# An expert's first layer begun with 128 rows, behind filler products, in an mLSTM and hash-routed mixture kernel

## Chip, cores and metric

The kernel runs on one core of a Trainium2 chip. The time is that of the whole program on the device, in microseconds: 430.01 us before the change, the median of three runs (429.15 to 430.22).

## What is computed

Two blocks follow each other. The first is an mLSTM cell over 4 batches, 8 heads and 768 time steps, with head dimension 40. Its output becomes a matrix x of 3072 rows (tokens) and 320 columns. The second sends each row to one of 8 experts by a hash of its token id; an expert is two matrix products with a relu between.

```python
def _moe_ref(x, token_ids, w1, w2):
    expert_idx = token_ids * np.int64(2654435761) % np.int64(E)
    for e in range(E):
        mask = expert_idx == e
        xe = x[mask]
        h = np.maximum(xe @ w1[e], 0.0)   # 320 -> 1024
        out[mask] = h @ w2[e]             # 1024 -> 320
```

All values are float32.

## The kernel before

**Attention.** The 3072 rows are worked in 24 blocks of 128 time steps (NT = 24, `s` in the loop), chunk by chunk with a carried state. TensorE (PE) makes the scores (L351), the part from the state (L402) and the part from the block (L409), and the transposes back (L424, tile xo). `finish(s)` normalises a block: VectorE (DVE) makes a denominator (L430, L433), multiplies by the output gate (L436, the last reader of xo in PSUM), takes a reciprocal (L439), and GpSimd (POOL) multiplies (L440). Then the sync queue stores 128 rows of x to DRAM (L441). Routing tables, which say what token lies in what slot of what expert, are made beside it.

**Experts.** Each of 8 experts takes 416 slots (CAP): three tiles of 128 rows and 32 of a remainder tile, `xr`, which four experts share. `fetch(e)` gathers rows of x from DRAM with an indirect DMA issued by POOL (L790), one for each tile, 3 for an expert and a fourth for xr at experts 0 and 4. As the rows were written by attention, the first gather waits for the last store. `turns(e)` is a list of four pieces: three that transpose a tile (`turn`, L806 on: two transposes L810, a small VectorE copy of the last 64 columns, L811, a third transpose L812, and a copy from PSUM to xT by VectorE, L816, or ScalarE, L814), and `remainder`, which at expert 0 transposes xr into `remT` (copied by ScalarE) and then copies 32 of its columns into xT on POOL (L896).

`layer1` goes over the 1024 hidden columns in four pairs of 128 (`fp`). Each has four whole matmuls (L834; 128 rows of w1, two for each half of the pair) and two halves (L827; the last 64 rows of w1, packed so that two run side by side in the array's row halves), into two PSUM tiles `mh`, of which there are four. VectorE evicts one with a relu (L841), ScalarE the other (L843). An fp32 matmul appears as two passes in the trace, so the eight passes of a pair's whole matmuls are one group. `layer2` multiplies h with w2 (L863, tile zp), and each 128 rows are copied by ScalarE (L796) and scattered by POOL (L797). Between the pairs of `layer1` and the tiles of `layer2` the function `between` is called: it puts the turns of the next expert into PE's order, and the issue of expert 2's weights (`third`, on ScalarE's queue).

The order of the work is written out by hand: each engine runs its instructions in the order in which the program names them, and semaphore waits are derived from the tiles. For expert 0 all four turns stand ahead of `layer1`. The PSUM pools of attention and of the experts use the same banks, so the first tiles of the second wait for readers of the first.

Of the kernel before, what the change touches and what calls it, by code (L numbers as in the profile page):

```python
# [8 lines left out]
F32 = mybir.dt.float32  # L9
# [4 lines left out]
AF = mybir.ActivationFunctionType  # L14
ALU = mybir.AluOpType
PSUM = bass.MemoryType.PSUM

P = 128
# [4 lines left out]
def kernel(  # L23
# [24 lines left out]
    nc = tc.nc  # L48
    B, H, S, D = q.shape
# [4 lines left out]
    E, _, F = moe_w1.shape  # L54
    FB = F // P
    NT = N // P
    PR = H // 2
# [9 lines left out]
    RM = 32  # L67
    EG = P // RM
    NM = NJ * P
    CAP = NM + RM  # L70
# [11 lines left out]
    ident = consts.tile([P, P], F32, name="ident")  # L82
# [20 lines left out]
    W = {}  # L103
# [13 lines left out]
    with tc.tile_pool(name="gates", bufs=1) as gp, \  # L117
# [308 lines left out]
        def finish(s):  # L426
            d = st.pop(s)
            hs = d["xo"].rearrange("p f i (x d) -> p f (i x) d", d=DP)
            den = wk.tile([P, 2, PR, 1], F32, name="den")
            nc.vector.tensor_scalar(  # L430
                den[:], hs[:, :, :, D:D1], scalar1=-1.0, scalar2=1.0, op0=ALU.mult, op1=ALU.max,
            )
            nc.vector.tensor_tensor(den[:], den[:], hs[:, :, :, D:D1], op=ALU.max)  # L433
            x = wk.tile([P, H, D], F32, name="x")
            xv = x.rearrange("p (j f) d -> p f j d", f=2)
            nc.vector.tensor_tensor(  # L436
                xv, hs[:, :, :, :D], og[s].rearrange("p (j f) d -> p f j d", f=2), op=ALU.mult,
            )
            nc.vector.reciprocal(den[:], den[:])  # L439
            nc.gpsimd.tensor_tensor(xv, xv, den[:].to_broadcast([P, 2, PR, D]), op=ALU.mult)  # L440
            return lambda: nc.sync.dma_start(x_d[s * P : (s + 1) * P, :], x.rearrange("p h d -> p (h d)"))  # L441


# [168 lines left out]
        one = gp.tile([P, 2, 1], F32, name="one")  # L612
# [174 lines left out]
    mps = ctx.enter_context(tc.tile_pool(name="mps", bufs=2, space=PSUM))  # L787

    def gather(xg, idx):
        nc.gpsimd.indirect_dma_start(  # L790
            out=xg, out_offset=None, in_=x_d[:, :], in_offset=bass.IndirectOffsetOnAxis(ap=idx, axis=0),
        )
# [13 lines left out]
    def turn(xg, dst, on_act):  # L806

        tp = mps.tile([P, DB, P], F32, name="tp")
        for db in range(2):
            nc.tensor.transpose(tp[:, db, :], xg[:, db * P : (db + 1) * P], ident[:])  # L810
        nc.vector.tensor_copy(xg[:, Dm:], xg[:, 2 * P : Dm])  # L811
        nc.tensor.transpose(tp[:, 2, :], xg[:, 2 * P :], ident[:])  # L812
        if on_act:
            nc.scalar.copy(dst, tp[:])  # L814
        else:
            nc.vector.tensor_copy(dst, tp[:])  # L816

    def layer1(w, xT, h, cols, between=lambda fp: None):

        w1t, w1c, _ = w  # L820
        for fp in range(FB // 2):
            hp = [mps.tile([P, CAP], F32, name="mh", bufs=4) for _ in range(2)]

            def halves(first):
                for i in range(2):
                    r = slice(i * P // 2, (i + 1) * P // 2)
                    nc.tensor.matmul(  # L827
                        hp[i][:, :cols], lhsT=w1c[r, fp, :], rhs=xT[r, 2, :cols], start=first, stop=not first,
                    )

            def whole(i, first):
                fb = 2 * fp + i
                for db in range(2):
                    nc.tensor.matmul(  # L834
                        hp[i][:, :cols], lhsT=w1t[:, db, fb * P : (fb + 1) * P], rhs=xT[:, db, :cols],
                        start=(first and db == 0), stop=(not first and db == 1),
                    )

            def out(i):
                if i == 0:  # L840
                    nc.vector.tensor_relu(h[:, 2 * fp, :cols], hp[i][:, :cols])  # L841
                else:
                    nc.scalar.activation(h[:, 2 * fp + 1, :cols], hp[i][:, :cols], AF.Relu)  # L843

            if fp % 2 == 0:
                for i in range(2):
                    whole(i, True)
                between(fp)
                halves(False)
                for i in range(2):  # L850
                    out(i)
            else:
                halves(True)
                for i in range(2):
                    whole(i, False)
                    out(i)
                between(fp)
# [12 lines left out]
    def cols_of(t, c0):  # L870
        return lambda j: t[:, c0 + j : c0 + j + 1]

    with tc.manual_schedule():
        xgs, xTs, remT, hrem = {}, {}, {}, {}

        def fetch(e):
            if e % EG == 0:
                xgs[-1 - e // EG] = xp.tile([P, DB * P], F32, name="xr")
            xgs[e] = xp.tile([P, NJ, DB * P], F32, name="xg", bufs=3)
            for j in range(NJ):  # L880
                gather(xgs[e][:, j, :Dm], cols_of(g_idx, e * NJ)(j))
            if e % EG == 0:
                gather(xgs[-1 - e // EG][:, :Dm], cols_of(g_idx, NR + e // EG)(0))

        def turns(e):
            xT = xTs[e] = xp.tile([P, DB, CAP], F32, name="xT")

            def tile_of(j):
                turn(xgs[e][:, j, :], xT[:, :, j * P : (j + 1) * P], j % 2 == 1)

            def remainder():
                i = e % EG
                if i == 0:
                    remT[e // EG] = xp.tile([P, DB, P], F32, name="remT")
                    turn(xgs[-1 - e // EG], remT[e // EG][:], True)
                nc.gpsimd.tensor_copy(xT[:, :, NM:], remT[e // EG][:, :, i * RM : (i + 1) * RM])  # L896

            return [lambda j=j: tile_of(j) for j in range(NJ)] + [remainder]

        def rest(g):  # L900
            zp = mps.tile([P, Dm], F32, name="zp")
            for fb in range(FB):
                for i in range(EG):
                    nc.tensor.matmul(
                        zp[i * RM : (i + 1) * RM, :], lhsT=hrem[g][:, i, fb, :], rhs=W[g * EG + i][2][:, fb, :],
                        start=(fb == 0), stop=(fb == FB - 1),
                    )
            scatter(zp, cols_of(s_idx, NR + g)(0), True)

        fetch(0)  # L910
        fetch(1)

        third = weight_slices(2)
        for piece in turns(0):
            piece()
        for e in range(E):
            g, i = e // EG, e % EG
            if e + 2 < E:
                fetch(e + 2)
            h = xp.tile([P, FB, CAP], F32, name="h")  # L920
            if i == 0:
                hrem[g] = xp.tile([P, EG, FB, RM], F32, name="hrem")
            ahead = turns(e + 1) if e + 1 < E else []

            def one(_):
                if ahead:
                    ahead.pop(0)()
                for _ in range(3):
                    if third:
                        third.pop(0)(nc.scalar)  # L930

            def after(j):
                one(j)
                if j == 0 and i == EG - 1:
                    rest(g)

            layer1(W[e], xTs[e], h, CAP, one)
            nc.gpsimd.tensor_copy(hrem[g][:, i], h[:, :, NM:])  # L938
            layer2(W[e], h, NJ, cols_of(s_idx, e * NJ), True, after)
            if e + 3 < E:  # L940
                load_weights(e + 3)

    nx = nc.values_load(xe[0:1, NX : NX + 1], min_val=0, max_val=NX)
    with tc.If(nx > 0):
        with tc.For_i(0, nx, 1) as k:
            ex = nc.sync.value_load(xe[0:1, bass.ds(k, 1)], min_val=0, max_val=E - 1)
            gs = xp.tile([P, 2], I32, name="gs")
            nc.vector.tensor_copy(gs[:, 0:1], g_idx[:, bass.ds(k + (NC - NX), 1)])
            nc.vector.tensor_copy(gs[:, 1:2], s_idx[:, bass.ds(k + (NC - NX), 1)])
            w, slices = weights(  # L950
                moe_w1[bass.ds(ex, 1)].rearrange("e d f -> (e d) f"),
                moe_w2[bass.ds(ex, 1)].rearrange("e f d -> (e f) d"), wpools[0], w2pools[0],
            )
            for piece in slices:
                piece()
            xr = xp.tile([P, DB * P], F32, name="xr")
            xT = xp.tile([P, DB, CAP], F32, name="xT")
            h = xp.tile([P, FB, CAP], F32, name="h")
            gather(xr[:, :Dm], gs[:, 0:1])
            turn(xr, xT[:, :, :P], False)  # L960
            layer1(w, xT, h, P)
            layer2(w, h, 1, lambda j: gs[:, 1:2], False)


# [28 lines left out]
```

## Time and profile before

The profiled execution has a span of 427.9 us. Busy times:

| engine | busy us | share |
|---|---|---|
| PE (matmul) | 386.1 | 90% |
| PEld (weight load, beside PE) | 258.5 | 60% |
| DVE | 136.1 | 32% |
| ACT (ScalarE) | 134.6 | 31% |
| POOL | 118.7 | 28% |

The page cuts the span into 40 slices and gives each engine's busy share in tenths, and the clock that PE was granted (9 is full). The chain that ended last is followed back from the last instruction, through what released each. Groups have a line, an engine, an output and its inputs, and the mean duration of one; a duration of a matmul includes its way through the array, so that successive ones overlap and their distance, not their duration, is their cost. "issue" is time in which an engine waited for nothing that the profile shows.

Expert 0's layer 1 stands between 173 and 198 us of the span. Of the costliest groups, the whole matmuls of `layer1` (L834) take 98.9 us in 256 passes, those of `layer2` (L863) 105.2 us in 384, the halves (L827) 26.7 us in 128.

### The profile page before, as it was taken

How to read it: one execution, taken by the hardware profiler on the slowest of the kernel's cores; microseconds unless marked ns; L12 is line 12 of the kernel's file. 1: busy time of each engine (PE TensorE's matmuls, PEld its weight loads, DVE VectorE, ACT ScalarE, POOL GpSimd, SP SyncE). 2: the span in 40 equal slices, each digit the busy share in tenths (PEclk: the TensorE clock that was granted, in tenths of full speed). 3: DMA queues.
4: the chain of work that ended last, by engine and by line, in shares of the span. 5: the costliest groups of instructions: out<-in, count | busy, mean ns of one | idle time of the engine just before them, and what ended most of it. 6: DMA issues, size and time to landing. Idle time of an engine off the chain costs nothing.

```text
span 427.9 us, 7402 instructions
## 1 busy us (share of the span) xinstructions
PE 386.1 (90%) x2862; PEld 258.5 (60%) x2862; DVE 136.1 (32%) x371; ACT 134.6 (31%) x238; POOL 118.7 (28%) x204
## 2 busy tenths in 40 slices
PE   2369999999999992599999999999999999999992
PEld 2257867877887871356656557556556566575551
DVE  7464748766675761211020120110110210201100
ACT  5158776686495471011010110110111111111010
POOL 6363323313323422710321501302302312021021
PEclk9868999999999998589999999999999999999997
DMA  8929998899676720527616318235216201000000
GB/s 168 213 61 172 206 218 180 190 205 214 149 161 129 161 90 33 163 96 239 193 46 212 120 29 271 62 98 170 75 64 214 61 8 38 0 15 31 1 17 30
DMA packets 111784, 51.37 MB, mean 120 GB/s; under 512 B 86624, under 2 KB 105892, under 8 KB 111748
## 3 DMA queue, kind: packets, MB, share of 16 engines
q1 hardware_dynamic: 105898, 39.31, 38.2%
q0 software_dynamic: 2496, 8.20, 6.0%
q10 hardware_dynamic: 3354, 3.37, 2.4%
q8 instruction: 23, 0.38, 0.4%
q14 instruction: 13, 0.11, 0.1%
HBM read 42.00 MB, written 8.63 MB: 118 GB/s over the span
## 4 chain that ended last, share of the span: by engine, by line
PE 78%; issue 5%; ACT 5%; DMA 4%; POOL 2%; DVE 1%; SPq 1%; ACTq 0%; POOLq 0%; DVEq 0%
PE mh L834 22%; PE zp L863 21%; PE mh L827 6%; PE sp L351 6%; PE ht L409 6%; PE ht L402 3%; PE ab L311 2%; PE tr L275 2%; PE xo L424 2%; PE ht L382 2%; PE tk L588 1%; PE tp L810 1%; ACT qT L289 1%; PE xb L323 1%; PE tr L288 1%
## 5 line engine op out<-in xcount | busy, mean ns | idle before, releaser
L863 PE MATMUL zp<-w2t,h 128*128 128x320 f32 x384 | 105.2, 433 | 0.0
L834 PE MATMUL mh<-xT,w1t 128*128 128x416 f32 x256 | 98.9, 531 | 0.9 <-POOL xT L896 0.9
L863 PEld LDWEIGHTS zp<-w2t,h 128*128 128x128 f32 x384 | 72.7, 190 | 32.1 <-issue 3.3
L834 PEld LDWEIGHTS mh<-xT,w1t 128*128 128x128 f32 x256 | 47.8, 194 | 44.0 <-issue 41.6
L816 DVE COPY xT<-tp 128x384 f32<-128x384 f32 x16 | 8.9, 558 | 142.3 <-PE tp L812 124.7
L797 POOL DMA_INDIRECT out_dram<-zo,s_idx x26 | 25.6, 986 | 92.5 <-ACT zo L796 92.5
L843 ACT ACTIVATE h<-mh 128x416 f32<-128x416 f32 x32 | 16.6, 517 | 110.1 <-PE mh L827 60.3
L796 ACT COPY zo<-zp 128x320 f32<-128x320 f32 x26 | 11.1, 426 | 101.1 <-PE zp L863 92.9
L841 DVE TENSOR_SCALAR h<-mh 128x416 f32<-128x416 f32 x32 | 18.9, 592 | 53.4 <-PE mh L834 26.9
L359 DVE TENSOR_TENSOR w<-sp,w 128x512 f32<-128x512 f32 x48 | 30.9, 686 | 13.8 <-PE sp L351 10.3
L440 POOL TENSOR_TENSOR x<-x,den 128x320 f32<-128x320 f32 x24 | 17.4, 724 | 64.0 <-DVE den L439 34.1
L351 PE MATMUL sp<-qT,kT 64*128 64x128 f32 x384 | 29.7, 297 | 4.1 <-ACT qT L289 4.1
L351 PEld LDWEIGHTS sp<-qT,kT 64*128 64x128 f32 x384 | 24.9, 199 | 10.8 <-ACT qT L289 6.0
L315 ACT ACTIVATE w<-ab 128x512 f32<-128x512 f32 x48 | 26.6, 611 | 5.0 <-PE ab L311 4.9
L409 PE MATMUL ht<-w,v 128*64 128x128 f32 x384 | 27.1, 285 | 0.0
L827 PE MATMUL mh<-xT,w1c 64*128 64x416 f32 x128 | 26.7, 535 | 0.0
L938 POOL COPY hrem<-h 128x256 f32<-128x256 f32 x8 | 3.2, 400 | 84.1 <-ACT h L843 84.1
L790 POOL DMA_INDIRECT xg<-x_rows,g_idx x24 | 23.4, 976 | 9.7 <-issue 9.7
L417 ACT COPY hT<-ht 128x512 f32<-128x512 f32 x24 | 14.1, 587 | 31.2 <-PE ht L409 31.2
L409 PEld LDWEIGHTS ht<-w,v 128*64 128x64 f32 x384 | 21.2, 140 | 4.0 <-issue 3.1
L289 ACT COPY qT<-tr 128x512 f32<-128x512 f32 x24 | 22.9, 975 | 0.6 <-PE tr L288 0.3
L275 PE MATMUL tr<-ident,k 128*128 128x128 f32 x96 | 17.2, 307 | 4.3 <-DMA k<-in_k_dram 4.3
(177 smaller groups left out, 407.0 us busy)
## 6 DMA issues: line engine op xcount, KB each, us to landing
w2t<-in_moe_w_dram SPq DMA_DIRECT2D x28, 320.0 KB
w1t<-in_moe_w_dram SPq DMA_DIRECT2D x28, 256.0 KB
k<-in_k_dram SPq DMA_DIRECT2D x24, 160.0 KB
v<-in_v_dram SPq DMA_DIRECT2D x24, 160.0 KB
og<-in_o_gate_dram SPq DMA_DIRECT2D x24, 160.0 KB
x_rows<-x SPq DMA_DIRECT2D x24, 160.0 KB
ql<-in_q_dram SPq DMA_DIRECT2D x6, 480.0 KB
w1c<-in_moe_w_dram SPq DMA_DIRECT2D x14, 128.0 KB
```

What stands on the lines that cost most here:

```text
L275: nc.tensor.transpose(tp[:, j, :], d["k"][:, 2 * j : 2 * j + 2, :].rearrange("p h d -> p (h d)"), ident[:])
L289: nc.scalar.copy(qb[b]["T"][:, :, cols], tp[:])
L315: nc.scalar.activation(w[:, hf], ab[:], AF.Exp)
L351: nc.tensor.matmul(sp[hf][:, j, :], lhsT=d["kT"][r, j, :], rhs=q_of(s)[r, j, :], start=True, stop=True,)
L359: nc.vector.tensor_tensor(d["w"][:, hf], d["sp"][hf][:], d["w"][:, hf], op=ALU.mult)
L409: nc.tensor.matmul(place(j, hf), lhsT=d["v"][:, 2 * j + hf, :], rhs=d["w"][:, hf, j, :], start=(c == 0 and j0 == 0), stop=True, skip_group ...
L790: nc.gpsimd.indirect_dma_start(out=xg, out_offset=None, in_=x_d[:, :], in_offset=bass.IndirectOffsetOnAxis(ap=idx, axis=0),)
L797: ins = nc.gpsimd.indirect_dma_start(out=out[:, :], out_offset=bass.IndirectOffsetOnAxis(ap=idx, axis=0), in_=zo[:], in_offset=None, bound ...
L827: nc.tensor.matmul(hp[i][:, :cols], lhsT=w1c[r, fp, :], rhs=xT[r, 2, :cols], start=first, stop=not first,)
L834: nc.tensor.matmul(hp[i][:, :cols], lhsT=w1t[:, db, fb * P : (fb + 1) * P], rhs=xT[:, db, :cols], start=(first and db == 0), stop=(not fir ...
L841: nc.vector.tensor_relu(h[:, 2 * fp, :cols], hp[i][:, :cols])
L863: nc.tensor.matmul(zp[:], lhsT=h[:, fb, j * P : (j + 1) * P], rhs=w[2][:, fb, :], start=(fb == 0), stop=(fb == FB - 1),)
```

## The change

Three things are changed at the passage from attention to experts.

- Eleven products of the identity with 416 columns of expert 0's weights are put into PE's order behind the last transposes of attention, into a PSUM tile `mh` that nobody reads. They are there to fill PE's gap.
- Expert 0's `layer1` is run twice: first over columns 0 to 127 of xT, for which only the first tile is turned beforehand, with the turns of tiles 1 and 2 and of xr put between its pairs; then over columns 128 to 415, with the turns of expert 1 and the issue of expert 2's weights between its pairs, as before. The 32 remainder columns of expert 0 are copied by VectorE straight from PSUM instead of by POOL from remT.
- The last block's multiply by the reciprocal (L440) is given to VectorE instead of POOL.

```diff
-            nc.gpsimd.tensor_tensor(xv, xv, den[:].to_broadcast([P, 2, PR, D]), op=ALU.mult)
+            eng = nc.vector if s + 1 == NT else nc.gpsimd
+            eng.tensor_tensor(xv, xv, den[:].to_broadcast([P, 2, PR, D]), op=ALU.mult)
...
-    def layer1(w, xT, h, cols, between=lambda fp: None):
+    def layer1(w, xT, h, c0, c1, between=lambda fp: None):
...
-                        hp[i][:, :cols], lhsT=w1t[:, db, fb * P : (fb + 1) * P], rhs=xT[:, db, :cols],
+                        hp[i][:, c0:c1], lhsT=w1t[:, db, fb * P : (fb + 1) * P], rhs=xT[:, db, c0:c1],
...
-                    turn(xgs[-1 - e // EG], remT[e // EG][:], True)
+                    tp = turn(xgs[-1 - e // EG], remT[e // EG][:], True)
+                if e == 0:
+                    nc.vector.tensor_copy(xT[:, :, NM:], tp[:, :, :RM])
+                    return
...
-        for piece in turns(0):
-            piece()
+
+        idle = mps.tile([P, CAP], F32, name="mh", bufs=4)
+        for _ in range(11):
+            nc.tensor.matmul(idle[:], lhsT=ident[:], rhs=W[0][0][:, 0, :CAP], start=True, stop=True)
+
+        first = turns(0)
+        first.pop(0)()
         for e in range(E):
...
-            layer1(W[e], xTs[e], h, CAP, one)
+            if e == 0:
+                layer1(W[e], xTs[e], h, 0, P, lambda fp: first.pop(0)() if first else None)
+            layer1(W[e], xTs[e], h, P if e == 0 else 0, CAP, one)
```

More of the change, by code (lines that the diff above doesn't have):

```diff
@@ L816, in turn @@
             nc.vector.tensor_copy(dst, tp[:])
-    def layer1(w, xT, h, cols, between=lambda fp: None):
+        return tp
+    def layer1(w, xT, h, c0, c1, between=lambda fp: None):
         w1t, w1c, _ = w
@@ L827, in halves @@
                     nc.tensor.matmul(
-                        hp[i][:, :cols], lhsT=w1c[r, fp, :], rhs=xT[r, 2, :cols], start=first, stop=not first,
+                        hp[i][:, c0:c1], lhsT=w1c[r, fp, :], rhs=xT[r, 2, c0:c1], start=first, stop=not first,
                     )
@@ L840, in out @@
                 if i == 0:
-                    nc.vector.tensor_relu(h[:, 2 * fp, :cols], hp[i][:, :cols])
+                    nc.vector.tensor_relu(h[:, 2 * fp, c0:c1], hp[i][:, c0:c1])
                 else:
-                    nc.scalar.activation(h[:, 2 * fp + 1, :cols], hp[i][:, :cols], AF.Relu)
+                    nc.scalar.activation(h[:, 2 * fp + 1, c0:c1], hp[i][:, c0:c1], AF.Relu)
             if fp % 2 == 0:
@@ L960 @@
             turn(xr, xT[:, :, :P], False)
-            layer1(w, xT, h, P)
+            layer1(w, xT, h, 0, P)
             layer2(w, h, 1, lambda j: gs[:, 1:2], False)
```

## The prediction

> **What bounds the kernel now.** I read the page's slices first, then the chain that ended last around the hole, the windows of the granted clock, and single groups for prices. In the slices (one is 10.7 us) TensorE is full but for the first three, the last, and slices 15 and 16; there the clock drops too.
>
> ```profile
> PE   2369999999999992599999999999999999999992
> PEclk9868999999999998589999999999999999999997
> ```
>
> From 179.17 on the chain is matmuls almost without a break, and from 210 to 418 us PE is busy 208.00 of 208.00 us. So what the hole between attention and expert 0 loses goes into the end time one for one. The chain through that hole (start, us, what):
>
> ```profile
> 162.91 0.79 PE ht L409 x14
> ...
> 166.50 0.73 POOL x L440
> 167.24 1.77 DMA x_rows<-x
> 170.02 1.19 POOL xg L790
> 171.51 0.95 POOL xg L790
> 172.77 0.95 POOL xg L790
> 174.02 3.24 DMA xr<-x_rows,g_idx
> 178.31 0.49 ACT remT L814
> 178.85 0.27 POOL xT L896
> 179.17 5.74 PE mh L834 x8
> 185.23 1.60 PE mh L827 x8
> 194.87 2.99 PE mh L834 x8
> 197.86 0.27 PE zp L863
> ```
>
> PE's last attention transposes end at 165.08; layer 1 begins at 179.17, released by the copy behind the fourth gather (xr); layer 2 begins at 197.86. The first eight passes take 5.74 us, where expert 1's eight take 2.79. The windows (columns: us, PE, PEld, DVE, ACT, POOL busy, granted clock, DMA) say why: the clock halves at about 167.55 and is back at 184.5, 5.3 us after dense work began.
>
> ```profile
> 167.00:167.50 0.50, 0.00 (x0) 0.00 (x0) 0.00 (x0) 0.00 (x0) 0.21 (x1) 1.00 0.04 16
> 167.50:168.00 0.50, 0.00 (x0) 0.00 (x0) 0.00 (x0) 0.00 (x0) 0.00 (x0) 0.53 0.00 0
> 184.00:184.50 0.50, 0.50 (x2) 0.23 (x1) 0.00 (x0) 0.00 (x0) 0.00 (x0) 0.50 0.30 113
> 184.50:185.00 0.50, 0.50 (x4) 0.25 (x2) 0.00 (x0) 0.00 (x0) 0.00 (x0) 0.90 0.00 0
> ```
>
> Two losses, then: four gathers' wait where one tile would let PE begin, and 18.69 us (179.17 to 197.86) for a layer that expert 1 does in 15.75 (210.78 to 226.53), so 2.94 of cold clock.
>
> [...] down 2.5 us after PE's last work, up 5.3 us into dense work. [...] transposes from 173.3 to 178.3 did not bring the clock back. [...] six passes of 128x47 (L588, below) step by 0.116 us[...].
>
> **The change part by part.** *Products.* In the built order the first of 11 waits for VectorE's multiply L436 of the last block, which ended at 165.47 + 0.48 = 165.95; PE stands from 165.08 to about 166.02[...], and the clock was still 1.00 at 167.5. Each fp32 product is two passes; at full clock eight passes take 2.79, so 0.349 each, and 22 take 7.67: PE is free again at about 173.69. Queued behind them is all of expert 0.
>
> *VectorE for the last x.* L440 ran on POOL from 166.50 to 167.23 and began 0.43 us after the reciprocal ended (166.06). The multiply L436 of the same size took 0.49 us on VectorE[...], so it ends near 166.6 and store and gathers start 0.6 to 0.7 us earlier. The first gather landed at 173.3, now about 172.65. But the products end at 173.69: this edit is hidden behind them, and is worth nothing. Equally the products overshoot the gather by 1 us, which I count as paid.
>
> *First tile.* From its first transpose to the start of the copy took 0.60 us at full clock (213.41 to 214.01, expert 2's first tile), the copy 0.56, semaphores 0.05: layer 1 starts at 173.69 + 1.21 = 174.90, instead of 179.17: 4.27 us earlier, and warm.
>
> *Layer 1 in two.* Expert 1's 15.75 us consist of 32 passes in groups of 2.79, 2.99, 2.80, 2.99 (11.57, so 0.349 a pass and 0.2 at two seams), two groups of halves at 1.60 (eight row pairs at 0.40, so 0.053 over a pass), and three turns at 0.33. No pass of 128 weights columns and 128 moving ones is in the trace outside transposes, so I bound it:
>
> ```profile
> 121.52 0.87 PE L588 MATMUL tk<-oh_c,oh_r 128*128 128x47 f32 x6
> 122.68 0.60 PE L288 MATMUL tr<-ident,qp 128*128 128x128 f32 x4
> ```
>
> With the mean of one (0.288, 0.272) taken off, the six step by 0.58 / 5 = 0.116 and the four transposes, which load and stream 128 columns, by 0.33 / 3 = 0.11. The stream itself is 0.349 x 128 / 416 = 0.107. Low end 0.109[...]. I take 0.116, since the four transposes are of this very shape.
> 128 rows: 32 x 0.116 = 3.71, seams 0.4, eight pairs at 0.116 + 0.053 = 1.35, three turns (tiles 1, 2, xr) 0.99; sum 6.45, ending at 181.35.
> 288 rows: a pass is 0.349 x 288 / 416 = 0.242; 32 x 0.242 = 7.74, seams 0.4, eight pairs at 0.295 = 2.36, expert 1's three turns 0.99; sum 11.49. Layer 2 begins at 192.84 instead of 197.86: 5.0 us earlier.
>
> *What is hidden.* Tiles 1, 2 and xr land at about 173.8, 175.0 and 176.6 (before: 174.4, 175.6, 177.26, less 0.65), and PE reaches their turns at about 175.9, 178 and 179.2. The 288 rows need the xT copies of tiles 1, 2 and the tail: ScalarE's copy of remT ends near 180.2, then the new 96-element VectorE copy (about 0.2; it takes the place of POOL's 0.27) near 180.45, against PE's 181.35. VectorE's queue mixes relus with the xg copies that the turns' last transposes need; the closest is tile 2, whose copy stands behind two relus: at most 0.1 us. Eight more relus on each of two engines (0.3 us each by L841's 0.59 for 416) lie beside PE. ScalarE now issues expert 2's weights from about 181.5 instead of 178.3; they are not read before expert 1 is through, some 38 us later. POOL's order shifts only behind gathers.
>
> Sum: 430.0 - 4.27 - 0.75 = 425.0, where 0.75 is 2.94 of cold clock saved less 2.19 for splitting (6.45 + 11.49 - 15.75).
>
> **The rivals.**
> *A, loads don't hide under 128-column streams.* [...] 425.0 + 3.9 = 428.9. For it: no such pass in the trace. Against it: the transposes' 0.11.
> *B, one cold window.* A window with PE's idle 0.94 us in it might still halve the clock for 3.4 us: 1.7 more, 426.7. Against it: from 160.7 to 164.1 PE had idle stretches of 0.74 us twice and kept 1.00.
> *C, slower.* Short passes and turns don't keep the clock: the 128 rows run at half rate (some 11.4 instead of 6.45) and the 288 rows stay cold for 5.3 us more (2.65 lost): 7.6 more, 432.6. A pass that is not pipelined at all (0.288, L588's full length) does nearly the same: 32 x 0.172 + 8 x 0.172 = 6.9 more, 431.9. For it: turns interrupt the short part[...]. Against it: attention is made of such short passes throughout and shows clock 9 or 1.00.
>
> **How the numbers follow.** Forecast 0.74, B 0.10, A 0.09, C 0.07. Time 425.0. Below it: no seams in the short part and pairs as cheap as passes (0.4 + 0.4), passes at 0.109 (0.2), and the 0.9 us by which the lowest run of before (429.15) lies under its median: 423.1. Above: B and a part of the way to A, 428.0, which leaves out A and C, 0.16. Faster by 0.3% (below 428.7) takes the forecast, B and half of A: 0.89; same 0.05; slower 0.06.
>
> **What would show it.** PEclk at 1.00 from 162 to 195; products from 166.0 to 173.7; first layer-1 pass near 174.9; groups of eight 128-column passes near 0.95 us; groups of 288 near 1.95; layer 2 from 192.8; the rest unchanged and shifted. I am wrong if the eight short passes take 1.7 or more (A), if the clock column falls under 1 after 167 (B, C), or if PE waits at a turn for VectorE or a gather, or later for expert 2's weights.

## The result and the profile after

The changed kernel took 431.66 us (median of four runs, 431.33 to 432.31) against 429.86 for the kernel before (median of four runs too): a ratio of 1.0046, with a 95% interval of 1.0028 to 1.0064. Forecast were 425.0 us, in a range of 423.1 to 428.0, so the time lies outside the range and on the wrong side. The ratios here are worked out from all fast runs, without the one slow run of the kernel before (441.33 us, beside the fourth measurement), and so are not the quotients of the medians.

That measurement doesn't stand alone. The same kernel, unchanged, was measured three more times, on three different chips, with the kernel before beside it each time. It took 425.62, 427.41 and 425.16 us, with ratios of 0.9899, 0.9939 and 0.9927. In the first measurement it is slower, in the three later ones faster and inside the range. On which chip the first measurement ran is not on record. Both have to be explained, and what follows reads them against each other.

The slices of the page of the first measurement, to be held against those of before:

```profile
PE   3368999998999988689999999999999999999992
PEclk9989999999999999969999999999999999999997
```

The hole in slices 15 and 16 (counted from 0) is gone, as meant, but a smaller one has opened in slice 16, one slice before the clock dips. The chain that ended last (start, us, what), from the products to layer 2 of expert 0:

```profile
166.54 7.92 PE mh L922 x22
...
175.44 1.16 PE mh L836 x8
...
177.57 1.09 PE mh L836 x8
178.66 0.22 PE tp L811 x2
178.87 2.75 issue
181.63 0.33 PE tp L813
...
182.85 1.18 PE tp L811 x2
...
184.77 0.47 PE tp L813
185.25 1.16 PE mh L829 x8
186.40 4.64 PE mh L836 x16
...
200.59 12.92 PE zp L865 x48
```

Up to 178.87 all is near the forecast: 22 passes of products in 7.92 us, the first eight short passes in 1.16 us, the next in 1.09. Then PE stands for 2.75 us at the third transpose (L813, formerly L812) of the second turn between the pairs, that of tile 2, and between 182.85 and 184.77 a second time, at the third of them, that of xr. Layer 2 begins at 200.59. From there to the end both kernels take 230.0 us (430.6 - 200.59; 427.9 - 197.86). Of the 2.7 us between the two spans, 2.3 are made in the stretch from attention's last transposes to here (35.06 against 32.78); the rest, 0.45, lies ahead of it.

What PE stood for is seen in VectorE's timeline of that trace (start, us, engine, line, what; in brackets the idle time ahead and what ended it):

```profile
181.17 0.29 DVE L843 TENSOR_SCALAR h<-mh 128x128 f32<-128x128 f32 x1 [3.50 <-remote]
181.38 0.20 DVE L812 COPY xg<-xg 128x64 f32<-128x64 f32 x1
184.06 0.56 DVE L817 COPY xT<-tp 128x384 f32<-128x384 f32 x1 [2.48 <-PE tp L811]
```

The second relu reads the first half of the second pair, whose four passes started at 177.50 and were over near 178.2. It started at 181.17, although VectorE had been idle for 3.50 us and the relu waits for PE's semaphore alone. ("Remote" says that the profile found no instruction behind the release; in the fourth trace, below, it names PE's L836.) The column copy of tile 2 (L812, formerly L811) stands behind it in VectorE's queue, and PE's third transpose waits for that copy. The copy of tile 2 out of PSUM likewise started 2.1 us after its transposes (181.63 + 0.33 to 184.06). ScalarE shows it too:

```profile
183.31 0.28 ACT L845 ACTIVATE h<-mh 128x128 f32<-128x128 f32 x1 [5.57 <-PE tp L811]
```

Its matmuls were over at 178.66. So in this trace PE's completions reached the waiting engines 2 to 5 us late between 178 and 184 us, on two engines. The ends of matmuls are modelled in the profile, so it cannot tell a late signal from a late end; "late signal" stands for both here. In the other direction, from VectorE to PE, the handover was prompt: the copy L812 ended at 181.58 and PE went on at 181.63. A window behind the two stands (from and to in us; busy us of PE, its matmuls and its loads apart, of DVE, ACT and POOL; then the clock and the DMA's share and rate) shows what the standing did next:

```profile
184.00:186.00 2.00, 1.23 (x9) 1.01 (x9) 0.86 (x3) 0.48 (x1) 0.17 (x1) 0.50 0.00 0
```

The clock halves near 182.9 (to 0.50) and is back at 1.00 near 189.7. The same kernel's fourth measurement has in the chain:

```profile
166.64 7.92 PE mh L922 x22
...
175.53 1.16 PE mh L836 x8
...
178.75 0.22 PE tp L811 x2
178.97 0.15 PE tp L813
...
180.99 3.03 PE mh L836 x16
```

Here the third transpose of the turn of tile 2 takes 0.15 us instead of 0.11, so the wait is 0.04 us, and no clock is lost (1.00 from 178 to 180 and from 182 to 184). Its VectorE timeline:

```profile
178.34 0.29 DVE L843 TENSOR_SCALAR h<-mh 128x128 f32<-128x128 f32 x1 [0.58 <-PE mh L836]
```

The second relu starts about 0.1 us after its matmuls. The stage of all traces of these two kernels, from the end of attention's last transposes to the start of layer 2, taken from the chains:

| trace | transposes end | layer 1 starts | layer 2 starts | stage us |
|---|---|---|---|---|
| before | 165.08 | 179.17 | 197.86 | 32.78 |
| forecast | 165.08 | 174.90 | 192.84 | 27.76 |
| changed, first | 165.53 | 175.44 | 200.59 | 35.06 |
| changed, second | 164.49 | 176.09 | 194.11 | 29.62 |
| changed, third | 165.91 | 177.51 | 195.53 | 29.62 |
| changed, fourth | 165.63 | 175.53 | 193.56 | 27.93 |

### The profile page after: what moved, and what is told of

It reads as the page before. It is cut to its first block, busy times and chain, and to the rows that moved or that the text cites. A ratio compares the mean times of both kernels' runs of the same rounds, so it can differ in the third digit from the quotient of the medians.

```text
span 430.6 us, 7550 instructions
## 1 busy us (share of the span) xinstructions
PE 392.6 (91%) x2932; PEld 267.4 (62%) x2932; DVE 137.2 (32%) x377; ACT 135.4 (31%) x242; POOL 117.6 (27%) x202
## 4 chain that ended last, share of the span: by engine, by line
PE 80%; issue 5%; ACT 5%; DMA 2%; POOL 2%; DVE 2%; ACTq 1%; SPq 1%; POOLq 0%; DVEq 0%
PE mh L836 22%; PE zp L865 21%; PE mh L829 6%; PE sp L351 6%; PE ht L409 5%; PE ht L402 3%; PE tr L275 2%; PE ab L311 2%; PE xo L424 2%; PE mh L922 2%; PE ht L382 2%; PE tp L811 2%; PE tr L288 2%; PE tk L589 1%; ACT qT L289 1%
## 5 line engine op out<-in xcount | busy, mean ns | idle before, releaser
L836 PE MATMUL mh<-xT,w1t 128*128 128x416 f32 (+2 forms) x288 | 98.7, 488 | 0.7 <-issue 0.7
L836 PEld LDWEIGHTS mh<-xT,w1t 128*128 128x128 f32 x288 | 51.9, 196 | 40.1 <-issue 37.3
L845 ACT ACTIVATE h<-mh 128x416 f32<-128x416 f32 (+2 forms) x36 | 17.3, 480 | 110.9 <-PE mh L829 52.8
L843 DVE TENSOR_SCALAR h<-mh 128x416 f32<-128x416 f32 (+2 forms) x36 | 19.6, 544 | 58.7 <-PE mh L836 27.1
L441 POOL TENSOR_TENSOR x<-x,den 128x320 f32<-128x320 f32 x23 | 16.6, 723 | 61.2 <-DVE den L439 29.3
L829 PE MATMUL mh<-xT,w1c 64*128 64x416 f32 (+2 forms) x144 | 27.8, 506 | 0.0
L311 PE MATMUL ab<-R,L 128*64 128x512 bf16 x96 | 16.6, 410 | 5.6 <-DMA L<-input_pieces 2.6
```

Of the source, the lines that this page charges most:

```text
L311: nc.tensor.matmul(ab[i * HB : (i + 1) * HB], lhsT=Ls[b % 2][:, c * P + i * HB : c * P + (i + 1) * HB], rhs=R[:, i, hf::2, :], start=True, ...
L829: nc.tensor.matmul(hp[i][:, c0:c1], lhsT=w1c[r, fp, :], rhs=xT[r, 2, c0:c1], start=first, stop=not first,)
L836: nc.tensor.matmul(hp[i][:, c0:c1], lhsT=w1t[:, db, fb * P : (fb + 1) * P], rhs=xT[:, db, c0:c1], start=(first and db == 0), stop=(not fir ...
L843: nc.vector.tensor_relu(h[:, 2 * fp, c0:c1], hp[i][:, c0:c1])
```

## The experiments

Theory one: PE's completions are signalled late while POOL's later gathers are issued and land (177.6 to 184.3 in the first trace). Theory two: they are late only where PE stands at a turn whose column copy is queued behind a relu that waits for PE. A third theory came up after the first four runs: that the lateness belongs to the executions first measured, not to the kernel.

### Parts alone

The eleven products alone, put ahead of the four turns of the kernel before:

```diff
+        idle = mps.tile([P, CAP], F32, name="mh", bufs=4)
+        for _ in range(11):
+            nc.tensor.matmul(idle[:], lhsT=ident[:], rhs=W[0][0][:, 0, :CAP], start=True, stop=True)
         for piece in turns(0):
```

> The kernel before with the eleven products alone: all four turns still ahead of one layer 1 over 416 rows, the last multiply still on GpSimd. Both theories agree here: no short passes and no turn that stands behind a relu, so no late signals. Layer 1 starts at 179.2 as before and takes 15.75 us instead of 18.69 if the clock stays at 1.00 over the turns (173.7 to 179.2): 427.0. If the clock falls during the turns[...], 428.5 to 430.

Measured: 430.0 us against 430.22, ratio 0.9996 (0.9981 to 1.001): no change. The chain of its trace:

```profile
179.83 4.71 PE mh L834 x8
```

The products kept the clock through the gap (22 passes in some 7.9 us), but it fell at 179.8, when PE had done nothing but transposes for 3.4 us (1.04 us of them busy), and the first eight passes took 4.71 us, not 2.79. Here filling the gap was worth nothing, as another thin stretch followed. Whether transposes as such fail to hold the clock was not shown; they filled only 1.04 of the 3.4 us. The case where the clock falls during the turns is the one that came.

Without the products, the rest of the change kept:

```diff
-        idle = mps.tile([P, CAP], F32, name="mh", bufs=4)
-        for _ in range(11):
-            nc.tensor.matmul(idle[:], lhsT=ident[:], rhs=W[0][0][:, 0, :CAP], start=True, stop=True)
```

> The changed kernel without the eleven products: layer 1 of expert 0 starts near 174.3 with the clock at half. Theory one (TensorE's completions are signalled late while the later gathers are issued and land): the late signals at 178 to 184 are there too, and the time is 432 or more. Theory two (they come late only where TensorE runs ahead and stands at a turn whose column copy is queued behind a relu): slower passes leave the relu time to be done first, TensorE stands less, and the time is 429 to 430.

Measured: 426.87 us, ratio 0.993 (0.9908 to 0.9951). Both numbers expected were too high. The clock was half only to 180.9 (eight short passes in 2.08 us, later in 0.89), and the split alone takes most of the gain:

```profile
175.45 2.08 PE mh L836 x8
...
181.16 0.22 PE tp L811 x2
181.38 0.11 PE tp L813
```

PE passes the second turn without a wait; stage 29.72 us (166.21 to 195.93).

### Fewer gathers in flight, or the copies moved

```diff
-            if e + 2 < E:
+            if 0 < e < E - 2:
                 fetch(e + 2)
...
             nc.gpsimd.tensor_copy(hrem[g][:, i], h[:, :, NM:])
+            if e == 0:
+                fetch(2)
```

> The changed kernel with expert 2's three gathers issued after expert 0's remainder copy, so that GpSimd issues seven gathers and no ten by 178.5. Theory one (late signals go with gathers in flight): the second relu of the short part starts 1 to 3 us earlier than 181.17 and all signals are prompt from about 180.5, the clock stays at 1.00, and the time is 425 to 428. Theory two (the order of VectorE's queue): nothing changes, second relu at about 181.2, 431.7.

Measured: 425.74 us, 0.9908 (0.988 to 0.9937).

```diff
         first.pop(0)()
+        for xg in (xgs[0][:, 1, :], xgs[0][:, 2, :], xgs[-1]):
+            nc.vector.tensor_copy(xg[:, Dm:], xg[:, 2 * P : Dm])
```

and the same copies taken out of these three turns (the loop stands here for three calls of a helper that does the copy).

> The changed kernel with VectorE's three column copies for tiles 1, 2 and xr queued ahead of the relus, right behind the copy of the first tile, so that no turn of TensorE waits behind a relu that waits for TensorE. Theory two (order): no late signals, the short part ends near 181.5, clock 1.00, time 425.0. Theory one (gathers): TensorE passes the second turn without a stop, but its completions are still signalled 2 to 4 us late, so it stands at the reuse of a PSUM tile instead; the gain is 1 to 3 us, 429 to 430.5.

Measured: 425.77 us, 0.99 (0.9868 to 0.9932). Each of the two seemed to confirm its own theory, so the pair cannot tell them apart; what was missing was the changed kernel itself on the same chip. It went into the next four, which ran together.

> The changed kernel as it is, once more, on the chip on which the next three run. Late gathers and early copies each took the late signals away, but so did nothing else so far: the first trace of the changed kernel also lacks many semaphore records between 175 and 184 us, which the four later traces have. Theory two (order of VectorE's queue, with gathers in flight): TensorE stands at the second turn for 2 to 3 us again, the clock falls, 431.5. Theory three (the late signals belong to the executions first measured, not to the kernel): no stand of more than 0.3 us, layer 2 begins 27.8 us after attention's last transposes, 425 to 426.5.

Measured: 425.62 us against 429.85, ratio 0.9899 (0.9874 to 0.9924). There is no stand in its trace at the turn of tile 2:

```profile
179.52 0.15 PE tp L813
```

Theories one and two both fall as sufficient causes: ten gathers in flight and the old order of VectorE's queue are here too, and the signals are prompt.

> The changed kernel with the three column copies ahead of the relus, again, beside the changed kernel on one chip. Theory two: 425.5 here against 431.5 there. Theory three: within 0.5 us of the changed kernel, since the copies are off the path when signals are prompt.

Measured: 426.4 us, 0.9915 (0.9888 to 0.9942): the copies are off the path when signals are prompt.

```diff
-        for _ in range(11):
+        for _ in range(8):
```

on top of the early copies:

> Early copies and eight products instead of eleven. Products end 3 x 0.70 = 2.1 us earlier, near 171.6 on the first trace's scale, but the first tile lands at 172.6: the first turn starts 1.0 us earlier than with eleven if the clock stays (424.5 to 425), or the clock falls at the gap of 1 us and up to 1.7 us go (426.5).

Measured: 425.18 us, 0.9879 (0.9844 to 0.9913). Its interval overlaps that of the changed kernel, so no difference is shown. In its trace the clock was half for one window, from 175.9 us (the eight short passes at 177.81 took 1.85 us, those at 179.83 took 1.06).

```diff
-            eng = nc.vector if s + 1 == NT else nc.gpsimd
+            eng = nc.gpsimd
```

> The changed kernel with the last multiply of x back on GpSimd: gathers start 0.65 us later, all else as changed. By the prediction the products hide it: the same time as the changed kernel within 0.3 us. If the late signals hang on how TensorE's short part falls against the gathers (theory two), the stand at the second turn changes by as much as a microsecond or goes.

Measured: 425.7 us, 0.9914 (0.9885 to 0.9944), 0.1 us from the changed kernel beside it. The interval alone would not exclude 0.65 us, but the trace does: VectorE has the first tile's rows at 173.41, and the products end at 174.06. The prediction's claim that this edit is hidden behind the products holds.

### Late relus made on purpose

If late signals can't be called up, their effect can: VectorE work on a scratch tile that nobody reads was put where the first trace had its delays.

> The changed kernel as it is, a third time. If the late signals of the first measurement come back in some share of executions, some runs here stand near 431 and the trace shows TensorE standing for over 1 us at the second or third turn; if they belong to that measurement alone, all runs are between 424.5 and 428 as in the second measurement (425.62).

Measured: 427.41 us against 430.19, 0.9939 (0.9921 to 0.9957); no run above 428.18.

```diff
             def out(i):
+                if i == 0 and fp == 1 and c1 == P and busy is not None:
+                    for _ in range(5):
+                        nc.vector.tensor_tensor(busy[:], busy[:], busy[:], op=ALU.max)
```

> The changed kernel with five 512-column VectorE operations on a scratch tile (3.5 us) put ahead of the short part's second relu, so that this relu starts some 2.9 us after its matmuls are done, as in the first trace of the changed kernel. If a late relu there is what held TensorE, it stands for 2.6 to 2.9 us at the second turn here too, on prompt signals: 428.3 if the clock holds, 430 if it falls for one window. If such a stand is absorbed (by work that was waiting elsewhere), the time stays at 425.6.

Measured: 429.97 us, 2.6 above the changed kernel on this chip; ratio 1.0005 (0.9986 to 1.0023). The two numbers expected were built on 425.6; on this chip, where the changed kernel took 427.41, the same sums give 430.1 and 431.8. The stand is not absorbed; in the trace it lasts 2.68 us:

```profile
181.66 0.20 DVE h L846
181.86 0.11 DVE xg L812
...
182.01 0.33 PE tp L813
```

Relu, column copy, transpose: the chain runs through all three. Behind it this trace has one window of half clock as well (eight halves in 1.16 us and sixteen passes in 3.87, not 0.65 and 3.03), so that its stage is 4.4 us longer than the fourth trace's (32.34 against 27.93). The profiled run of the changed kernel on this chip lost as much clock elsewhere, in its products (22 passes in 9.61 us and not 7.92, so 1.7), which is why the two differ by less.

```diff
         else:
+            for _ in range(3 if busy is not None else 0):
+                nc.vector.tensor_tensor(busy[:], busy[:], busy[:], op=ALU.max)
             nc.vector.tensor_copy(dst, tp[:])
```

for tile 2, in addition:

> As before, and three more such operations (2.1 us) ahead of the copy of tile 2, which the third turn's column copy stands behind: both delays of the first trace. TensorE stands for 4.4 us in two places within one and a half clock windows, so the clock should fall as it did there: 4.4 us of standing and about 2.5 us of half clock on top of 425.6, 431.5 to 432.5. If the clock does not fall, 430.0.

Measured: 433.64 us, 6.2 above the changed kernel beside it, ratio to before 1.0073 (1.0051 to 1.0095). That is above the range expected, which was built on 425.6 again; 5.9 to 6.9 on top were expected. The first measurement lay 6.0 above the second. The chain has its sizes as well:

```profile
186.26 0.47 PE tp L813
186.73 1.16 PE mh L831 x8
187.89 4.94 PE mh L838 x16
```

against 0.47, 1.16 and 4.64 there. The profiled execution had, besides, a half-clock window in its products (9.61 us too), as had that of the changed kernel beside it.

### Once more, and the copies' place

> The changed kernel as it is, a fourth time. If the late signals depend on where it runs, some measurement should show them again: 431 or more, TensorE standing for microseconds at the turns. If the first measurement was alone in it: 425 to 427.5, as in the second and third.

Measured: 425.16 us against 429.29, 0.9927 (0.9899 to 0.9956). No stand.

> Early column copies and eight products, beside the changed kernel on one chip with more rounds. The products end 1.0 us ahead of the first tile's landing instead of 1.1 us behind it: 1 us faster than the changed kernel if the clock holds; equal, if the gap costs the clock a window of 1.7 us in half of the executions.

Measured: 425.28 us, 0.9913 (0.9887 to 0.9939). In its trace layer 1 starts 9.05 us after attention's transposes, not 9.90, but the timings don't tell it from the changed kernel, neither here nor in the run above. It isn't shown to be better than the change.

> The changed kernel with the column copies ahead of the relus and the second relu held up by the same 3.5 us of scratch operations that cost 2.6 us where the copies stood behind it. If the column copy's place in VectorE's queue is what lets a late relu stop TensorE, TensorE passes the second turn now, and at most 0.5 us is lost where the PSUM tile of that relu is used again: within 0.6 us of the changed kernel on this chip. If the relu holds TensorE in another way, 2.5 us or more above it.

Measured: 426.99 us, 0.9943 (0.9921 to 0.9966). By the medians this is 1.8 above the changed kernel on this chip, where up to 0.6 was expected; by the ratios it is 0.7 (0.9943 against 0.9927), with intervals that overlap. The same late relu with the copies behind it cost 2.8 by the ratios (1.0005 against 0.9939). The times point to the copies' place, then, but it is the traces that show it. The profiled execution had half clock in the products (22 passes in 9.61 us), which is 1.7 us of its time. From the first short pass to the end of the group of sixteen passes it took 9.11 us (176.72 to 185.83), the changed kernel 8.49 (175.53 to 184.02), and the kernel with the same late relu and the copies behind it 12.90 (175.89 to 188.79):

```profile
180.16 0.11 PE tp L817
...
182.80 3.03 PE mh L840 x16
```

The third transpose no longer waits. The 0.6 us are lost later, at the halves that reuse a PSUM tile. Of the 4.4 us between 12.90 and 8.49, 2.7 are the stand and the rest is the window of half clock behind it. So the place of the column copy behind the relu is what turns a late relu into a stand of TensorE.

## Why the prediction was right or wrong

**Right, by the traces.** Layer 1 starts 9.90 us after the transposes in the fourth trace, 9.82 forecast. It is that close only because three errors cancel: the products wait for the reciprocal (L439) and not for the multiply by the gate ahead of it (1.01 us, 0.94 forecast), they take 7.92 us and not 7.67, and the first tile's turn and copy take 0.97 and not 1.21. A pass of 128 by 128 steps by 0.11 us (eight in 0.89 where no seam falls among them, though the record of one lasts 0.28, so that records overlap; 0.116 taken, 0.109 as the low end), and eight with a seam take 1.16 or 1.09. Of the smaller prices, a relu of 128 columns takes 0.29 us on VectorE (0.3 taken) and the copy of 96 elements 0.26 (about 0.2). The groups of 288 take 1.94 to 2.14 (1.94 plus a seam). The stage lasts 27.93 us in the fourth trace and 27.88 with early copies, 27.76 forecast. Rival A, loads that don't hide, is out. No trace stood behind its price of a load. From the trace of before that can be estimated at 0.11 us at most, the distance of L588's loads:

```profile
121.52 0.74 PEld L588 LDWEIGHTS tk<-oh_c,oh_r 128*128 128x128 f32 x6 [0.17 <-issue]
```

One of them lasts 0.19 us, so the six start (0.74 - 0.19) / 5 = 0.11 us apart. With a stream of 0.107, the prediction's own estimate, a pass in series would have come to some 0.22 us and eight to over 1.7; they took 0.89 to 1.16. The VectorE edit is worth nothing, as said; the multiply takes 0.49 us there, as taken (L441 in the first trace of the changed kernel), and 0.72 on POOL (L440 before).

**Wrong: the step "what is hidden".** It said of VectorE's queue that "the closest is tile 2, whose copy stands behind two relus: at most 0.1 us". Behind this stood a term of the sum, "semaphores 0.05": that every completion reaches the engine that waits for it at once, as in the trace of before POOL's copy, which ended at 179.12, let PE go on at 179.17. In the first measurement the second relu came some 3 us after its matmuls, and the copy's place behind it cost 2.75 us. The same queue's next copy cost 1.70: from the first transpose of xr to the third it took 1.92 us (182.85 to 184.77), and 0.22 in the fourth trace. Each of these copies stood behind an instruction that waited for PE. The other part is clock: transpose, halves and the sixteen passes behind it took 0.47 + 1.16 + 4.64 instead of the fourth trace's 0.11 + 0.65 + 3.03, so 2.5 us. Together 7.0 of the 7.1 us between the two stages. In the other three measurements the step holds: 0.04 us in each trace.

What the step did wrong was to check a margin for its size on prompt signals and stop there. It found a circle of waits (PE waits for a copy, the copy for a relu queued ahead of it, the relu for earlier work of PE) and called it hidden since the sum came out 0.1 us short. Such a circle had hardly any slack here: a relu that was made 2.9 us late left TensorE standing for 2.68. The prediction named the sign, "if PE waits at a turn for VectorE", but gave it no price and no chance. C, the slower rival, named the clock, which did fall, but as a consequence of the stand. Where the signals were prompt, in three measurements, the time came out inside the forecast's range, though the gain was less than the 5.0 us forecast: 2.6 to 4.3 by the ratios.

**A chance that was too small.** Rival B, one half-clock window in the products, had 0.10. Of twelve traces with eleven products, five have it (22 passes in 9.61 us, not 7.92, so 1.7 as worked out), the second and third of the changed kernel among them. The second:

```profile
162.25:165.67 3.42, 1.66 (x21) 1.21 (x18) 1.14 (x7) 0.58 (x1) 0.72 (x1) 1.00 0.15 50
165.67:169.08 3.41, 3.41 (x6) 1.63 (x6) 0.32 (x1) 0.00 (x0) 0.30 (x1) 0.50 0.14 48
```

The changes of the granted clock lie on a grid of 3.41 us in each trace (before: 17.4, 24.2, 27.6, 34.4, 167.5, 184.6 and 423.6; the changed kernel's first: 29.3, 32.7, 182.9, 189.7 and 425.2), and the place of the grid differs from one execution to the next. PE stands twice here, 0.74 us for attention's last copy hT and 1.02 us ahead of the products, with the last transposes between. In the five traces one window of the grid holds both stands (PE is busy for 1.65 or 1.66 us of it), and the next is at half clock. In the other seven the grid cuts through one of them, PE is busy for 1.89 us or more in each window there, and the clock stays. This sorts the twelve traces, but it is no full rule: a window of the trace without products has 1.66 us as well (163.80 to 167.21), and the one behind it kept the full clock. The prediction weighed the second stand alone, though no trace had shown that so short a stand costs no clock, and its argument against B, "twice 0.74 us" from 160.7 to 164.1, counts too much: PE was busy for 2.28 us there, so it stood for 1.12 and not 1.48. Nor was the window idle behind which the clock fell before the change: from 164.12 to 167.53 PE was still busy for 0.66 us.

With half clock in the products the stage is 29.62 us, no shorter than without products at all (29.72, one trace). So by the traces the products bring up to 1.8 us when the clock holds and nothing when it doesn't, and the split carries the change; the times don't tell the kernels with and without products apart.

**What stays open.** Why PE's completions were late in the first measurement; the made delays show what lateness costs, not where it came from. All four of its runs were above 431 us; none of the 18 timed runs of the same kernel in the three later measurements was above 428.5. Its trace also holds some 290 fewer records of semaphores than the later traces of the same program (5,734 against 6,023), most of them among the landings of GpSimd's gathers and scatters. The trace of the kernel before, taken with it, lacks about as many of the DMA's landings, yet in that kernel no engine waits for a signal of PE between 178.4 and 184 us, and it lost nothing. That both come from one cause is a guess. Gathers in flight alone don't do it: they are in all later traces. Two rivals were not tested: the chip of the first measurement, to which no later run is known to have gone back, and the recording of events itself, from which records are missing in the same traces.

## What to carry to other kernels

When work is split so that an engine runs ahead, look for circles of waits in the queues: TensorE waiting for a copy that is queued behind a relu that waits for TensorE. Put instructions that depend only on data from memory ahead of those that wait for the engine you want to keep busy, even where the margin on paper suffices: here no cost of it was measured with prompt signals (ratios of 0.9915 with it and 0.9899 without, with intervals that overlap), and with a late relu it saved 3.8 us of 4.4 in the traces (2.1 of 2.8 by the ratios). And when a measured loss sits in one wait, run the unchanged kernel again beside the first remedies, or each remedy will seem to prove its own theory.

## What had not been expected of the hardware

In one measurement VectorE and ScalarE went on only 2 to 5 us after the passes of PE that they waited for, over some 6 us, while three later measurements of the same kernel show none of it. And two short stands of PE, 0.74 and 1.02 us, were followed by a window of half clock (22 passes in 9.61 us, not 7.92) when both fell into one window of 3.41 us (five of twelve traces), and not when they fell into two.
